# First maxima row on ScalarE's queue, half of the first q on GpSimd's, third head's q and two gate/up tiles further on

## The chip, the cores and the metric

The kernel runs on one core of one Trainium2 chip. The metric is the device time of one execution in microseconds (us). Three runs of the kernel before gave 1214.02, 1212.59 and 1212.71 us, a median of 1212.71. One further execution was profiled.

## The reference

What is computed, cut to what matters (2048 tokens, width 448, 16 heads of 28, hidden width 1792; all in float32):

```python
x = A_x                                             # (1, 2048, 448)
g = sigmoid((x * gate_w).sum(-1, keepdims=True))
q, k, v = split(x @ wqkv)                           # 16 heads of 28
a = softmax(q @ k.T * 28 ** -0.5) @ v @ wo          # per head, then joined
gate, up = x @ W_gate, x @ W_up                     # (2048, 1792)
b = (gate * (gate > 0) * up) @ W_down
return g * a + (1 - g) * b
```

## The kernel before

**Numbers.** Almost every matmul operand is split into a high part and the remainder (`act_high` and `low`: ScalarE casts, VectorE or GpSimd subtracts), and the products of the parts are accumulated, 11 matmuls (`NT`) for a full width of 448. A row block of 512 tokens is `tb` 0 to 3, and `X[tb]` holds its two parts, each a tile of 1 MB.

**Stages.** (1) Preparation: `qk` units project a block of q and k columns, and send both parts to the DRAM array `qk_d` (every second unit through the staging tile `K[2]`, the others through the tiles `rl` and `h`, all stores on GpSimd's queue). `load_k(h)` and `load_q(h)` bring one head back, q once for each of two halves of the rows and each of two parts, in four transfers of 224 KB. `vproj` units make V, and between their matmuls stand the matmuls of `smax`, which find the largest score of each query of heads 0 and 1, so that the later exponentials cannot overflow. `smax_end(h)` transposes these maxima, splits them into the two halves of the tile `mh`, and writes them as two rows into the head's q tile `Q[h]`: scores then come out with their maximum already subtracted. (2) Attention: 32 rounds, each an order string (`R0` to `R31`), in which each letter is one step: `s` a pair of score matmuls and ScalarE's copy or exponential of them, `m` an `smax`, `x` one matmul of a remaining qk unit or a gate/up unit, and so on. (3) The rest: `down` steps (12 matmuls each, one for each 128 hidden units and 512 tokens), the last `gate_up` tiles, the output projection `wout`, and the mix with the gate.

**What sets the order.** The schedule is by hand: every engine and every DMA queue runs its instructions in the order in which the code issues them, and a DMA on a queue waits for its data before those behind it can go. SP issues nearly all DMAs, POOL (GpSimd) the stores of the preparation and the spills.

**Preparation around the change.** The list `mixed` has 19 units: three `qk`, then 16 `vproj`, blocks 3 down to 0. At step `n` of it some side work is issued first: loads of heads 1 and 2, the splits of two pieces of the raw weights (`split_w(*w3)`, `split_w(*w2)`, four or two casts on ScalarE, the remainders on POOL), and `spill_x(tb, r)`, which stores one part of `X[tb]` to the DRAM array `x_d` by POOL's queue. The spills clear the way twice. The third q tile, `Q2`, lies where the second part of `X[3]` was, so the load of head 2's q waits for spill (3, 1). And the first score tiles `P` lie where the others were: slot 0 at (3, 0), slots 1 and 2 at (2, 0) and (2, 1), slots 3 and 4 at (1, 0) and (1, 1). `EARLY` places eight score pairs in the last five `vproj` units; the first four of these need no maxima, the fifth needs the row of head 0. `fetch_f` loads raw gate/up weights.

**End around the change.** Of the 56 gate/up tiles (14 for each block) the rounds do 52 (`done`), and the other four stand in the list `todo` of stage 3. Each reads weights (`wg`, two buffers of 896 KB) that were split once and are loaded again from DRAM (`ws_d`); `load_f(i + 2)` is issued when tile `i` is done. Its result goes to DRAM (`spill_h`), to be read by a `down` step of the fourth block. A `down` step reads the two parts of one hidden tile, `hh`, made by `split_d` from `hk` or `hr`.

Of the kernel before, what the change touches and what calls it, by code (L numbers as in the profile page):

```python
# [18 lines left out]
P = 128  # L19
# [3 lines left out]
DH = 28  # L23
G = 4
GD = G * DH
F = 1792
NF = F // P
NB = 4
# [83 lines left out]
def gated_mix_kernel(ctx, tc, x, wq, wo, wgu, wd, out):  # L112
    nc = tc.nc
# [7 lines left out]
    def f32(ap):  # L121
        return ap.bitcast(F32)
# [21 lines left out]
    def ps_x(name):  # L144
        return psum.tile([P, TB], F32, tag="x", bufs=2, name=name)
# [7 lines left out]
    def low(dst, src, high):  # L153
        nc.vector.tensor_tensor(dst, src, f32(high), op=OP.subtract)  # L154
# [5 lines left out]
    qk_d = dram.tile([2 * D, 2, S + P], F32, name="qk_d")[:, :, :S]  # L160
# [17 lines left out]
    def last_q(name, dt=F32R):  # L178
        return vp.tile([P, 4, TB], dt, name=name, tag="Q2", bufs=1)
# [9 lines left out]
    Q = {}  # L189

    def rows_kq(h):

        g, j = divmod(h, 4)
        k = 2 * GD * g + (DH * j if g else 2 * DH * j)
        return k, k + (GD if g else DH)

    def load_k(h):
        a = rows_kq(h)[0]
        k = qk_d[a:a + DH].rearrange("d r t -> (d r) t")
        for a in (0, 2 * DH):  # L200
            nc.sync.dma_start(f32(K[h % 3])[a:a + 2 * DH], k)

    def load_q(h):
        Q[h] = QS[h % 3].rearrange("p j t -> p (j t)")
        if h > 2:
            nc.sync.dma_start(f32(Q[h])[GD:GD + 2], f32(Q[h])[GD + 2:GD + 4])
        q = rows_kq(h)[1]
        for a in range(2):
            for r in range(2):
                nc.sync.dma_start(f32(Q[h])[2 * DH * a + r:2 * DH * (a + 1):2], qk_d[q:q + DH, a])  # L210

    MX, M = {}, {}
    def raw(v):
# [29 lines left out]
    def smax_end(h):  # L243

        pt = ps_x(f"mt_{h}")
        n = NU[h]
        nc.tensor.transpose(pt[:n, :P], M.pop(h), ident)
        mh = keep.tile([n, 2, P], F32R, name=f"mh_{h}", tag="mh", bufs=1)
        nc.scalar.activation(mh[:, 0], pt[:n, :P], AF.Copy)
        low(mh[:, 1], pt[:n, :P], mh[:, 0])  # L250
        for r in range(2):
            nc.sync.dma_start(f32(Q[h])[GD + r:GD + r + 1, :n * P], f32(mh)[:, r])

    AT, QUAD, slots = {}, {}, iter(range(10 ** 6))

# [104 lines left out]
    def fetch_f(i):  # L360

        if i >= NF:
            return
        WR[i] = fe.tile([P, 2, 4, P], F32, name=f"wgr_{i}", tag="wgr", bufs=2)
        nc.sync.dma_start(WR[i], wgu[i % NF])
# [10 lines left out]
    with tc.tile_pool(name="qkv", bufs=1) as pa:  # L376
        W = pa.tile([P, 7, VO + VC], F32R, name="W")

        def load_w(c):
            c0, c1 = c * 2 * GD, (c + 1) * 2 * GD if c < G + 1 else 2 * D + VC  # L380
            wr = pa.tile([P, 4, 2 * GD + 2], F32, name=f"wr_{c0}", tag="wr", bufs=2)[:, :, :c1 - c0]
            if c > 0:
                nc.sync.dma_start(wr, wq[:, :, c0:c1])
            return wr, c0, c1

        def split_w(wr, c0, c1, low=low):

            n, k = c1 - c0, VO - 2 * GD
            if c0 == 2 * GD:
                ways = [(W[:, :, c0:VO], wr[:, :, :k]), (WB[0][:, :, :n - k], wr[:, :, k:])]  # L390
            elif c0 == 4 * GD:
                k = 2 * P - (c0 - VO)
                ways = [(WB[0][:, :, 2 * P - k:], wr[:, :, :k]), (WB[1][:, :, :n - k], wr[:, :, k:])]
            elif c0 == 6 * GD:
                ways = [(WB[1][:, :, 2 * P - n:], wr)]
            else:
                ways = [(W[:, :, c0 - 2 * D + VO:c1 - 2 * D + VO], wr)]
            for w, r in ways:
                act_high(w[:, 0:3], r[:, 0:3])
                low(w[:, 3:6], r[:, 0:3], w[:, 0:3])  # L400
            for w, r in ways:
                act_high(w[:, 6], r[:, 3])
                low(w[64:, 6], r[64:, 3], w[64:, 6])
# [39 lines left out]
        def spill_x(tb, r):  # L443
            nc.gpsimd.dma_start(x_d[tb, r], f32(X[tb][r]))
# [95 lines left out]
        split_w(*w4)  # L540
        load_k(0)
        load_q(0)

        mixed = [(qk, 3, 1), (qk, 2, 2), (qk, 3, 2)]
        mixed += [(vproj, tb, t) for tb in range(NB - 1, -1, -1) for t in range(4)]
        spills = dict(zip((7, 8, 9, 10, 11, 12, 14, 16), ((3, 0), (2, 0), (2, 1), (1, 0), (3, 1), (1, 1), (0, 0), (0, 1))))
        m, first, ahead = 0, 6, MAXIMA
        for n, (f, *a) in enumerate(mixed):
            if n == 0:
                split_w(*w5)  # L550
            if n == 1:
                w3 = load_w(3)
            if n == 2:
                load_k(1)
                load_q(1)
            if n == 3:
                w2 = load_w(2)
            if n == 4:

                nc.gpsimd.memset(f32(K[2])[96:128], -1.0)  # L560
            if n == 7:
                load_k(2)
            if n == 8:
                split_w(*w3, pool_low)
            if n == 10:
                split_w(*w2, pool_low)
            if n == 13:
                QS.append(last_q("Q2"))
                for i, j in ((GD, 12), (GD + 12, 4)):
                    nc.sync.dma_start(f32(QS[2])[i:i + j].rearrange("p j t -> p (j t)"), Q[1][GD + 2:GD + 2 + j].bitcast(F32))  # L570
                load_q(2)
            if n == len(mixed) - 6:
                fetch_f(0)
                fetch_f(1)
            if n in spills:
                spill_x(*spills[n])

            among, was = [], m
            while n >= first and m < (n + 1 - first) * ahead / (len(mixed) - first):
                among.append((smax, m))  # L580
                m += 1
            news = [(score,) for back in EARLY if back == len(mixed) - n]
            for k, c in enumerate(news):
                among.insert(2 * k + 1, c)
            f(*a, among=among)

            if 0 in M and was > ends[0]:
                smax_end(0)
# [18 lines left out]
    done = (starts[-1] - QP) // (2 * NT)  # L607
# [178 lines left out]
    for v, order in enumerate(ROUNDS):  # L786
# [4 lines left out]
        for o in order:  # L791
# [12 lines left out]
            elif o == "x":  # L804
                i, half, n = passes.pop(0)
# [18 lines left out]
            elif o == "n":  # L824
                if v % 2 and v < 2 * H - 1:
                    smax_end(v // 2 + 1)
            elif o == "w":
                ready = -(-max(0, starts[v + 2] - QP) // NT)
                ready = min(ready + ready % 2, 2 * NF)
                while parts < ready and parts // 2 - 2 in finished:  # L830
                    split_f(parts // 2, act_high, pool_low, (parts % 2,))
                    parts += 1
                    if parts % 2 == 0:
                        fetch_f(parts // 2 + 1)
            elif o == "b":
                block_min()
            elif o == "A":
                all_max()
            elif o == "g":
                take_max()  # L840
            elif o == "N":
                if v > 1 and v % 2:
                    normalise(v // 2 - 1)
            elif o in "eE":
                take_exp(o == "E")
            elif o in "cf":
                rescale(v, "cf".index(o))
            elif o == "D":
                split_wd(len(early))
                early.append(o)  # L850
            elif o in "PQ":
                pv(v, "PQ".index(o))
# [10 lines left out]
    def load_wo():  # L863
        r = pf.tile([P, 4, TB], F32, name="wor", tag="on0", bufs=2)
        nc.sync.dma_start(r[:, 0:3, :D], wo_d[0:3 * P].rearrange("(c p) n -> p c n", p=P))  # L865
        for a in (0, 64):
            nc.sync.dma_start(r[a:a + 64, 3, :D], wo_d[3 * P:])  # L867
        return r[:, :, :D]
# [82 lines left out]
    def down(i):  # L951
# [6 lines left out]
        if f == NF - 1:  # L958
# [8 lines left out]
    todo = [(fetch_w, 4), (fetch_h, 4), (fetch_w, 5), (fetch_h, 5), (split_d, 0), (row_sums, H - 1), (split_d, 1),  # L967
            (fetch_w, 6), (fetch_w, 7), (lambda: wor.append(load_wo()),), (fetch_h, 6), (gate_up, done), (spread, H - 1),
            (split_wd, 4), (fetch_w, 8), (split_wd, 5), (fetch_w, 9), (fetch_h, 7), (gate_up, done + 1)]
    for i in range(NB * NF):  # L970
        if 5 < i + 3 < NF:
            todo += [(split_wd, i + 3), (fetch_w, i + 7)]
        if i + 2 < NB * NF:
            todo.append((split_d, i + 2))
        if i >= 2:
            todo.append((fetch_h, i + 6))
        todo.append((down, i))
        if done + 2 + i < NB * NF:
            todo.append((gate_up, done + 2 + i))

    def before(i, *new):
        n = todo.index((down, i))
# [51 lines left out]
```

## Time and profile before

| | |
|---|---|
| median of three runs | 1212.71 us |
| the profiled execution | 1216.88 us |
| its span, first to last instruction | 1215.0 us |
| mean granted TensorE clock | 0.990 |
| TensorE (PE) busy | 1188.5 us |
| VectorE (DVE) busy | 896.1 us |
| ScalarE (ACT) busy | 878.8 us |
| GpSimd (POOL) busy | 741.5 us |
| DMA | 188.86 MB, mean 155 GB/s |

The profile gives one execution. A timeline row has start, duration, engine, line, operation, output and input, count, and in brackets how long the engine was idle ahead of it and what ended that. SPq, ACTq and POOLq are DMA issues on those engines' queues. A line such as "PE s L341 <- DMA Q<-mh" says that TensorE's matmul of tile `s` in line 341 waited for the DMA that writes `Q` from `mh`. Names leave buffer numbers out. The clock column is the share of the full TensorE clock that was granted.

### The profile page before, as it was taken

To read this page: it belongs to the slowest core of one execution; us is meant where nothing else is said; L and a number is where in the kernel's file an instruction comes from. 1 tells how busy PE (TensorE), PEld (TensorE's weight loads), DVE (VectorE), ACT (ScalarE), POOL (GpSimd) and SP (SyncE) were. 2 spreads that over 40 slices of the span, in tenths; PEclk is the share of its full clock that TensorE was granted. 3 is DMA by queue.
4 is the path that set the end of the run, shared out by engine and by line. 5 is a ranking of instruction groups with operands and counts; after the bars stand their busy time and mean duration, and the time that the engine had idled before them with its cause. 6 is when DMAs were issued, how large, how long until landed. Compare 5 with 4: busy or idle time off the path is not lost. (4 is left out here: it accounts for less than half of the span.)

```text
span 1215.0 us, 16951 instructions
## 1 busy us (share of the span) xinstructions
PE 1188.5 (98%) x6183; PEld 824.6 (68%) x6183; DVE 896.1 (74%) x1173; ACT 878.8 (72%) x1018; POOL 741.5 (61%) x323
## 2 busy tenths in 40 slices
PE   9996999999999999999999999999999998999998
PEld 6784666666666666666666566666666665899987
DVE  5484888888888888989888898989888551443342
ACT  5234788999999888888888888888888983422121
POOL 5320767789888777767776766667687773321020
PEclk9997999999999999999999999999999998999999
DMA  8983555754454645343446435153544337543342
GB/s 307 271 329 115 183 178 178 233 166 156 148 149 156 191 139 149 109 134 109 126 119 215 124 115 156 40 156 98 161 128 156 125 119 240 155 147 111 121 126 77
DMA packets 70655, 188.86 MB, mean 155 GB/s; under 512 B 13946, under 2 KB 20546, under 8 KB 65666
## 3 DMA queue, kind: packets, MB, share of 16 engines
q1 hardware_dynamic: 65756, 167.78, 44.9%
q0 software_dynamic: 4384, 19.53, 4.3%
q8 instruction: 49, 0.80, 0.3%
q10 hardware_dynamic: 432, 0.46, 0.1%
q14 instruction: 34, 0.28, 0.1%
HBM read 126.96 MB, written 60.96 MB: 155 GB/s over the span
## 5 line engine op out<-in xcount | busy, mean ns | idle before, releaser
L320 POOL TENSOR_TENSOR P<-P,rm 128x2048 f32<-128x2048 f32 x102 | 470.6, 4633 | 117.9 <-DVE rm L314 85.1
L644 PE MATMUL gu<-X,wg 128*128 128x512 f32 x1232 | 366.2, 399 | 5.8 <-DMA wg<-ws_d 5.8
L239 DVE TENSOR_REDUCE mx<-sm 128x1 f32<-128x1024 f32 x256 | 304.5, 1217 | 71.2 <-PE sm L235 69.2
L341 PE MATMUL s<-Q,K 128*128 128x512 f32 x1024 | 320.7, 403 | 12.6 <-DMA Q<-mh 10.9
L644 PEld LDWEIGHTS gu<-X,wg 128*128 128x128 f32 x1232 | 232.1, 189 | 77.2 <-issue 19.6
L341 PEld LDWEIGHTS s<-Q,K 128*128 128x128 f32 x1024 | 182.7, 188 | 92.1 <-issue 17.1
L347 ACT ACTIVATE P<-s 128x1024 f32<-128x1024 f32 x204 | 202.0, 1028 | 39.6 <-PE s L341 37.1
L703 PE MATMUL po<-P,V 128*32 128x512 f32 x1640 | 229.9, 595 | 0.0
L345 ACT ACTIVATE P<-s 128x1024 f32<-128x1024 f32 x206 | 201.8, 1032 | 28.6 <-PE s L341 26.7
L331 ACT ACTIVATE P<-P 128x1024 f32<-128x1024 f32 (+1 forms) x154 | 202.1, 1344 | 1.4 <-POOL P L320 1.1
L291 DVE SCALAR_TENSOR_TENSOR r<-s,r 128x1024 f32<-128x1024 f32 x124 | 151.8, 1224 | 20.8 <-ACT P L347 10.2
L235 PE MATMUL sm<-K,Q 128*128 128x512 f32 x520 | 161.4, 399 | 2.2 <-DMA Q<-qk_d 2.1
L703 PE MATMUL po<-V 128*32 128x512 f32 x408 | 136.8, 594 | 0.0
L703 PEld LDWEIGHTS po<-P,V 128*32 128x32 f32 x1640 | 60.8, 109 | 110.6 <-issue 107.4
L320 POOL TENSOR_TENSOR V<-V,rm 128x2048 f32<-128x2048 f32 x24 | 111.2, 4634 | 23.1 <-DVE rm L314 12.2
L235 PEld LDWEIGHTS sm<-K,Q 128*128 128x128 f32 x520 | 94.2, 189 | 34.5 <-issue 5.0
L148 ACT ACTIVATE hh<-hr 128x512 fp32r<-128x512 f32 x52 | 32.7, 631 | 113.2 <-PE acc L938 111.0
L154 DVE TENSOR_TENSOR hh<-hr,hh 128x512 fp32r<-128x512 f32 x52 | 45.2, 875 | 78.2 <-ACT hh L148 78.2
L938 PE MATMUL acc<-WD,hh 128*128 128x448 f32 x480 | 100.1, 366 | 0.4 <-DVE hh L154 0.3
L938 PEld LDWEIGHTS acc<-WD,hh 128*128 128x128 f32 x480 | 90.0, 188 | 8.7 <-DVE hh L154 1.2
L306 DVE TRANSPOSE_TENSOR_REDUCE mn<-r 128x32 f32<-128x1024 f32 x63 | 77.9, 1237 | 1.2
L291 DVE SCALAR_TENSOR_TENSOR r<-s,P 128x1024 f32<-128x1024 f32 x50 | 61.2, 1223 | 23.6 <-ACT P L347 23.1
(92 smaller groups left out, 1136.4 us busy)
## 6 DMA issues: line engine op xcount, KB each, us to landing
wg<-ws_d SPq DMA_DIRECT2D x42, 896.0 KB
K<-qk_d SPq DMA_DIRECT2D x32, 448.0 KB
Q<-qk_d SPq DMA_DIRECT2D x64, 224.0 KB
X<-x_d SPq DMA_DIRECT2D x56, 256.0 KB
h_d<-h SPq DMA_DIRECT2D x56, 256.0 KB
hr<-h_d SPq DMA_DIRECT2D x52, 256.0 KB
ws_d<-wg SPq DMA_DIRECT2D x14, 896.0 KB
x_d<-X POOLq DMA_DIRECT2D x8, 1024.0 KB, 10.5
```

The source lines that it names most:

```text
L235: nc.tensor.matmul(ps[:, c, :], Q[h][:, u * P:(u + 1) * P], K[h % 3][:, k0:k0 + TB], start=True, stop=True)
L239: nc.vector.tensor_reduce(to, ps, axis=AX.XY, op=OP.max)
L291: nc.vector.scalar_tensor_tensor(r, ps, -1.0, before, op0=OP.mult, op1=OP.min)
L306: nc.vector.tensor_reduce(MN[:, 1:3], R2.pop((v, j)).rearrange("p a (b r) -> p a b r", r=32), axis=AX.X, op=OP.min, apply_transpose=True)
L320: nc.gpsimd.tensor_tensor(QUAD[q], QUAD[q], m, op=OP.subtract)
L331: nc.scalar.activation(q, q, AF.Exp, scale=-SCALE)
L341: nc.tensor.matmul(ps[:, c], K[h % 3][:, k * P:(k + 1) * P], Q[h][:, j * TB:(j + 1) * TB], start=True, stop=True)
L345: nc.scalar.activation(dst, ps, AF.Exp, scale=SCALE)
L347: nc.scalar.activation(dst, ps, AF.Copy, scale=-1.0)
L644: nc.tensor.matmul(ps, WS[i][:, s, a], xf(i // NF, b), start=(n == 0), stop=(n == NT - 1))
L703: nc.tensor.matmul(po[32 * j:32 * j + 32], V[:, h // 4 % 2, k, h % 4], AT.pop((v, k, j)), start=(k == k0), stop=(k == k0 + NK // 2 - 1))
L938: nc.tensor.matmul(ACC[i // NF][t][:, :D], HH[i][:, a, t * P:(t + 1) * P], wd_high_low(f, b), start=(f == 0 and n == 0), stop=(f == NF - 1 ...
```

## The change

Five edits. The first head's q is loaded by two queues: its first half (`a` = 0, two of four transfers) by GpSimd, the second by SP. The two row transfers of `smax_end(0)` are issued by ScalarE's queue; those of later heads stay on SP. Spill (3, 1) becomes the second of the eight, and the last two come at steps 16 and 17 in place of 14 and 16. The side work moves on: the two weight splits from steps 8 and 10 to 12 and 14, the load of head 2's q from 13 to 17, `fetch_f` from 13 to 18. In stage 3 the last two gate/up tiles stand behind down steps 2 and 4 instead of 0 and 1.

```diff
@@ load_q
-                nc.sync.dma_start(f32(Q[h])[2 * DH * a + r:2 * DH * (a + 1):2], qk_d[q:q + DH, a])
+                queue = nc.sync if h or a else nc.gpsimd
+                queue.dma_start(f32(Q[h])[2 * DH * a + r:2 * DH * (a + 1):2], qk_d[q:q + DH, a])
@@ smax_end
-            nc.sync.dma_start(f32(Q[h])[GD + r:GD + r + 1, :n * P], f32(mh)[:, r])
+            (nc.sync if h else nc.scalar).dma_start(f32(Q[h])[GD + r:GD + r + 1, :n * P], f32(mh)[:, r])
@@ preparation
-        spills = dict(zip((7, 8, 9, 10, 11, 12, 14, 16), ((3, 0), (2, 0), (2, 1), (1, 0), (3, 1), (1, 1), (0, 0), (0, 1))))
+        spills = dict(zip((7, 8, 9, 10, 11, 12, 16, 17), ((3, 0), (3, 1), (2, 0), (2, 1), (1, 0), (1, 1), (0, 0), (0, 1))))
...
-            if n == 8:
+            if n == 12:
                 split_w(*w3, pool_low)
-            if n == 10:
+            if n == 14:
                 split_w(*w2, pool_low)
-            if n == 13:
+            if n == 17:
                 QS.append(last_q("Q2"))
...
-            if n == len(mixed) - 6:
+            if n == len(mixed) - 1:
                 fetch_f(0)
                 fetch_f(1)
@@ todo
-        if done + 2 + i < NB * NF:
-            todo.append((gate_up, done + 2 + i))
+        if i % 2 == 0 and 0 < i and done + 1 + i // 2 < NB * NF:
+            todo.append((gate_up, done + 1 + i // 2))
```

SP's queue in the preparation, from the load of head 0's q on (`Q_107`, `Q_108` and `Q_684` are the q tiles of heads 0, 1 and 2, `wr` raw weights of qk, `wgr` raw gate/up weights, `mh` the maxima), before:

```order
L210 DMA Q_107<-qk_d 28x2048 x4
L383 DMA wr_401<-wq 128x4x224
L201 DMA K_105<-qk_d 56x2048 x2
L210 DMA Q_108<-qk_d 28x2048 x4
L383 DMA wr_442<-wq 128x4x224
L201 DMA K_106<-qk_d 56x2048 x2
L570 DMA Q_684<-Q_108 12x2048
L570 DMA Q_684<-Q_108 4x2048
L210 DMA Q_684<-qk_d 28x2048 x4
L365 DMA wgr_691<-wgu 128x1024
L365 DMA wgr_693<-wgu 128x1024
L252 DMA Q_107<-mh_755 1x12x128 x2
```

The same place of the change (head 2's q is now `Q_810`, and line numbers behind 209 are one higher):

```order
L211 DMA Q_107<-qk_d 28x2048 x2
L384 DMA wr_401<-wq 128x4x224
L201 DMA K_105<-qk_d 56x2048 x2
L211 DMA Q_108<-qk_d 28x2048 x4
L384 DMA wr_442<-wq 128x4x224
L201 DMA K_106<-qk_d 56x2048 x2
L571 DMA Q_810<-Q_108 12x2048
L571 DMA Q_810<-Q_108 4x2048
L211 DMA Q_810<-qk_d 28x2048 x4
L366 DMA wgr_849<-wgu 128x1024
L366 DMA wgr_851<-wgu 128x1024
L375 DMA qk_d<-rl_qk_0_933 128x512
```

Two of head 0's q loads have gone to POOL's queue (there behind the last store that they read, ahead of the stores of the three mixed `qk` units), and the two rows of maxima to ScalarE's, behind its cast of `mh`; the rest keeps its order on SP.

POOL in the preparation, from the first spill on (`x_d_0_78<-X_3` is spill (3, 0), `x_d_1_79<-X_3` is (3, 1), and so on; `wb` are the weight splits, `v_d` the stores of V), before:

```order
L444 DMA x_d_0_78<-X_3_121 128x2048
L157 TENSOR_TENSOR wb_114<-wr_401,wb_114 128x3x224
L157 TENSOR_TENSOR wb_114<-wr_401,wb_114 64x224
L444 DMA x_d_0_76<-X_2_123 128x2048
L444 DMA x_d_1_77<-X_2_124 128x2048
L157 TENSOR_TENSOR wb_113<-wr_442,wb_113 128x3x192
L157 TENSOR_TENSOR wb_114<-wr_442,wb_114 128x3x32
L157 TENSOR_TENSOR wb_113<-wr_442,wb_113 64x192
L157 TENSOR_TENSOR wb_114<-wr_442,wb_114 64x32
L444 DMA x_d_0_74<-X_1_125 128x2048
L488 DMA v_d_80<-V 128x512
L488 DMA v_d_81<-V 128x512
```

And of the change:

```order
L445 DMA x_d_0_78<-X_3_121 128x2048
L445 DMA x_d_1_79<-X_3_122 128x2048
L445 DMA x_d_0_76<-X_2_123 128x2048
L445 DMA x_d_1_77<-X_2_124 128x2048
L489 DMA v_d_80<-V 128x512
L489 DMA v_d_81<-V 128x512
L445 DMA x_d_0_74<-X_1_125 128x2048
L157 TENSOR_TENSOR wb_114<-wr_401,wb_114 128x3x224
L157 TENSOR_TENSOR wb_114<-wr_401,wb_114 64x224
L445 DMA x_d_1_75<-X_1_126 128x2048
L157 TENSOR_TENSOR wb_113<-wr_442,wb_113 128x3x192
L157 TENSOR_TENSOR wb_114<-wr_442,wb_114 128x3x32
```

Four spills now stand in a row, and five stand ahead of the first split; the second split follows the sixth.

ScalarE at the beginning of stage 3 (`rl` is the relu of a gate/up tile, `hh` the cast for a down step, `WD` and `WO` casts of weights), from the relu of the second of the four tiles on, before:

```order
L660 ACTIVATE rl_9014<-gu_8989 128x512
L148 ACTIVATE hh_9020<-hk_8229 128x512
L660 ACTIVATE rl_9062<-gu_9039 128x512
L148 ACTIVATE hh_9068<-hk_8229 128x512
L148 ACTIVATE WO<-wor 128x1344
L148 ACTIVATE WO<-wor 128x448
L660 ACTIVATE rl_9115<-gu_9092 128x512
L148 ACTIVATE hh_9121<-hr_8918 128x512
L148 ACTIVATE WD<-wdr_8933 128x448
L148 ACTIVATE hh_9142<-hr_8922 128x512
```

And of the change:

```order
L661 ACTIVATE rl_9014<-gu_8989 128x512
L148 ACTIVATE hh_9020<-hk_8229 128x512
L148 ACTIVATE hh_9039<-hk_8229 128x512
L148 ACTIVATE WO<-wor 128x1344
L148 ACTIVATE WO<-wor 128x448
L148 ACTIVATE hh_9063<-hr_8918 128x512
L661 ACTIVATE rl_9103<-gu_9080 128x512
L148 ACTIVATE WD<-wdr_8933 128x448
L148 ACTIVATE hh_9113<-hr_8922 128x512
L594 ACTIVATE e<-zt 128x16
L148 ACTIVATE WD<-wdr_8935 128x448
L148 ACTIVATE hh_9139<-hr_8941 128x512
```

The third tile's relu now follows the casts of down steps 2, 3 and 4 in place of step 2's alone, and the fourth tile's stands behind these rows.

## The prediction

> **What bounds the kernel now.** I read the page first, then the waits of TensorE, then windows around each of its stops, then each queue's timeline there.
>
> ```profile
> span 1215.0 us, 16951 instructions
> ...
> PE 1188.5 (98%) x6183; PEld 824.6 (68%) x6183; DVE 896.1 (74%) x1173; ACT 878.8 (72%) x1018; POOL 741.5 (61%) x323
> ```
>
> TensorE is busy for 98% of the span, so an edit can pay only where TensorE stands still or is slowed. Its waits over the whole span name these places (engine, line, what it waited for: us in total, times, longest):
>
> ```profile
> PE s L341 <- DMA Q<-mh: 10.9, 1, 10.9
> PE gu L644 <- DMA wg<-ws_d: 5.8, 1, 5.8
> PE sm L235 <- DMA Q<-qk_d: 2.1, 1, 2.1
> PE warm_ps L507 <- DVE warm L504: 1.2, 1, 1.2
> ```
>
> Three waits hold 18.9 us; nothing else is above 1.2 us. Each of the three is touched by one part of the change. The windows show each wait, the matmuls behind it, and the same set of matmuls elsewhere (window, length, busy time and count of PE, PEld, DVE, ACT, POOL; then the granted clock, DMA share, GB/s):
>
> ```profile
> 46.16:48.30 2.14, 0.00 (x1) 0.03 (x1) 0.00 (x0) 0.00 (x0) 0.42 (x1) 1.00 0.87 323
> 48.30:52.29 3.99, 3.98 (x11) 3.43 (x12) 2.08 (x2) 0.00 (x0) 1.38 (x1) 0.57 1.05 272
> 57.20:59.56 2.36, 2.36 (x12) 2.07 (x11) 2.25 (x3) 0.26 (x1) 2.28 (x3) 1.00 0.99 206
> 91.22:102.15 10.93, 0.01 (x1) 0.03 (x1) 0.87 (x1) 0.00 (x0) 0.00 (x0) 0.59 0.74 220
> 102.15:107.41 5.26, 5.26 (x15) 4.41 (x15) 1.23 (x1) 1.47 (x2) 0.00 (x0) 0.55 0.00 0
> 107.41:110.44 3.03, 3.03 (x16) 2.63 (x15) 1.44 (x2) 2.10 (x4) 0.00 (x0) 1.00 0.00 0
> 1021.66:1027.49 5.83, 0.00 (x0) 0.03 (x1) 0.00 (x0) 0.00 (x0) 0.00 (x0) 0.79 1.04 348
> 1027.49:1034.69 7.20, 7.20 (x23) 5.71 (x23) 0.00 (x0) 0.00 (x0) 1.28 (x1) 0.70 0.78 255
> 1037.12:1042.28 5.16, 5.16 (x24) 4.14 (x23) 2.18 (x2) 0.57 (x2) 0.00 (x0) 1.00 0.32 91
> 300.00:900.00 600.00, 599.49 (x3255) 378.03 (x3257) 527.17 (x691) 526.97 (x566) 446.36 (x154) 1.00 0.45 137
> ```
>
> A wait costs twice. Behind each the clock is about 0.6, and the matmuls take longer than the like stretch at full clock: 3.99 - 2.36 = 1.63 us, 5.26 - 3.03 = 2.23 us, 7.20 - 5.16 = 2.04 us. So the first wait is worth 2.14 + 1.63 = 3.8 us, the second 10.93 + 2.23 = 13.2, the third 5.83 + 2.04 = 7.9. From 300 to 900 us TensorE is full at clock 1.00: what is gained in the preparation stays gained.
>
> **The row of maxima (second wait).** Head 0's first scores need the row `mh`. Its halves exist early and leave late (start, us, engine, line):
>
> ```profile
> 80.88 0.27 ACT L249 ACTIVATE mh<-mt 12x128 fp32r<-12x128 f32 x1
> ...
> 82.17 0.27 DVE L154 TENSOR_TENSOR mh<-mt,mh 12x128 fp32r<-12x128 f32 x1
> ...
> 81.99 2.21 SPq L570 DMA_DIRECT2D Q<-Q  x2
> 84.25 7.93 SPq L210 DMA_DIRECT2D Q<-qk_d  x4
> 92.23 1.47 SPq L365 DMA_DIRECT2D wgr<-wgu  x2
> 93.81 1.63 SPq L252 DMA_DIRECT2D Q<-mh  x2
> ...
> SPq L570 <- DMA x_d<-X: 28.1, 1, 28.1
> ```
>
> Done at 82.44, issued from 93.81 to 95.44: SP sat 28.1 us at the third head's buffer, which waited for a spill of X, then issued six DMAs for that buffer and two weight loads ahead of the row. On ScalarE's queue the row passes all eight. Two issues at SP's 0.8 us each end by 83.3; TensorE wants the row at 91.22, 7.9 us later. A row's landing on ScalarE's queue is not in this trace. On SP it took 102.15 - 95.44 = 6.7 us with two weight loads just ahead of it, which would do; the longest of the spills to DRAM is the bound above:
>
> ```profile
> DMA to landing us min/median/max: 4.3/10.5/14.7
> ```
>
> At 14.7 us TensorE would still wait 14.7 - 7.9 = 6.8 us and lose the slow stretch: 9 of the 13.2 us stay lost. Six KB sit nearest to the 6.7 us row, so I take no wait: **-13.2**. Cover: 7.9 us. What the issues hold up on ScalarE:
>
> ```profile
> 83.07 1.02 ACT L347 ACTIVATE P<-s 128x1024 f32<-128x1024 f32 x1 [1.92 <-PE s L341]
> ```
>
> It had waited 1.92 us for TensorE before 83.07; the second issue, held until 82.44, may delay this copy by 0.2 us, which that idle time absorbs for the next. It stands in the allowance below.
>
> **Head 0's q (first wait).** SP loads it behind K, in four issues; POOL issues the stores these loads wait for:
>
> ```profile
> 32.59 0.68 POOL L475 DMA_DIRECT2D qk_d<-K  x1 [1.99 <-DVE K L154]
> 34.41 0.56 POOL L374 DMA_DIRECT2D qk_d<-rl_qk  x1 [1.14 <-ACT rl_qk L148]
> ...
> 47.88 1.80 POOL L560 MEMSET K<- 32x2048 f32 x1 [7.12 <-DMA qk_d<-K]
> 53.33 1.07 POOL L488 DMA_DIRECT2D v_d<-V  x2 [3.65 <-ACT zt L485]
> ...
> 35.83 0.79 SPq L201 DMA_DIRECT2D K<-qk_d  x2
> 36.66 3.32 SPq L210 DMA_DIRECT2D Q<-qk_d  x4
> ```
>
> Two K loads of 448 KB and four of q at 224 KB, 1792 KB, are issued from 36 us and let TensorE go at 48.30: 12.3 us. With two q loads taken out, SP's share is 1344 KB: 9.2 us at that pace, 45.2, before TensorE's 46.16. POOL's pair must wait for the store issued at 32.59, so until about 35.8; with issues like its other 0.6 us ones it is out by 37.1. At the spills' median of 10.5 us it lands at 47.6, at their shortest of 4.3 at 41.4. Both directions are open: at 14.7 us (51.8) TensorE waits 3.5 us longer than now, at 9 us or less it waits for nothing. The pair is smaller than a spill and nothing is queued ahead of it on POOL's queue, so I take it as gone but for 0.3 us: **-3.5**. POOL's wait puts the store of 34.41 and those behind it back by up to 2.8 us; they feed the memset at 47.88, and the v_d store behind it has 3.65 us idle ahead of it, which covers that.
>
> The Trainium skill speaks against this part: DMA: Bandwidth & Descriptors, "Issuing engines are not separate DMA queues", says that transfers of all issuers share the same 16 engines and interleave, so a second issuer only saves issue time. The trace has DMA busy at 0.87 in the wait, which fits. By that rule the 3.8 us stay and the sum falls to 19.6 us; it is a rival below.
>
> **Third head's q, spills, splits.** Four issues of q, two copies and two weight loads now stand behind later code on SP, but their blocker, X's spill (3,1), moves from fifth to second on POOL and is no longer held behind the weight splits. Nothing needs that q before the second round string, nor the weight loads before the fourth; the last two spills, up to two steps later, free X for reloads that the first round issues only after its first four units. If that cover went, TensorE would wait for the rest of a transfer there. The two splits move four steps on; their first reader, at L652, comes at 110.90, some 30 us after. The risk is the second split's raw load:
>
> ```profile
> 69.97 1.23 ACT L148 ACTIVATE wb<-wr 128x576 fp32r<-128x576 f32 x4 [6.88 <-DMA wr<-wq]
> ...
> 76.16 0.55 ACT L484 ACTIVATE V<-v 128x448 f32<-128x448 f32 x1 [2.58 <-PE v L480]
> ...
> 78.79 1.03 ACT L347 ACTIVATE P<-s 128x1024 f32<-128x1024 f32 x1 [2.02 <-PE s L341]
> ...
> 64.00:68.00 4.00, 4.00 (x20) 3.52 (x19) 3.76 (x4) 0.00 (x0) 0.00 (x0) 1.00 0.94 393
> ```
>
> Now it lands at 69.97 amid three spills of 1 MB; then up to two more are ahead, each 1 MB / 393 GB/s = 2.7 us: 70 to 75.4. After the 3.5 us gained above, ScalarE must start the first score copy at 75.3, so the four casts (1.23 us) must start by 74.1. The cost lies between nothing and 75.4 - 74.1 = 1.3 us, more if the spills' overlap is worse; I take **+0.5** for this and the delayed copies. Behind the casts on ScalarE queue the copies that free PSUM, and for those TensorE waits.
>
> **Two gate and up tiles (third wait).**
>
> ```profile
> 1019.06 2.60 PE L938 MATMUL acc<-K,hh 128*128 128x448 f32 x12
> 1027.49 7.36 PE L644 MATMUL gu<-X,wg 128*128 128x512 f32 x22 [5.83 <-DMA wg<-ws_d]
> ...
> 1047.14 14.75 PE L938 MATMUL acc<-WD,hh 128*128 128x448 f32 x72
> ...
> 1019.50 0.38 SPq L629 DMA_DIRECT2D wg<-ws_d  x1
> ...
> 1020.50 0.68 DVE L154 TENSOR_TENSOR hh<-hk,hh 128x512 fp32r<-128x512 f32 x1
> ```
>
> One down step of 12 matmuls is 14.59 / 6 = 2.43 us (start 1047.14 to the next group at 1061.73). The tile whose weights land at 1027.49 now follows three steps, not one: 2 x 2.43 = 4.86 us of the 5.83 are filled. The third step reads the `hh` done at 1021.2, so it is ready. 0.97 us of wait stays, since the weights are still issued at 1019.50 behind the same DMAs. If the clock holds through that, the part is worth 7.87 - 0.97 = **-6.9**. The second moved tile's load and the stores moved behind it have two steps more, which hide them.
>
> **The sum**: 3.5 + 13.2 + 6.9 - 0.5 = 23.1 us. The profiled execution took 1216.88 us around a span of 1215.0, so it would take 1193.8. Its time is 4.2 us above the runs' median of 1212.71; I put the same gain on the median: **1189.6 us**.
>
> **The rivals.**
> (a) Head 0's q is bound by the DMA engines, and the first wait stays: 1189.6 + 3.5 = 1193.1. For it: share 0.87 and 323 GB/s in the wait. Against: POOL's pair now stands ahead of stores that competed with it.
> (b) The raw load of the second split is late: with all five spills ahead, twice 2.7 us more, 1.3 + 5.4 = 6.7 us at most, so 1190.4 to 1195.8. For: the 6.88 us wait it already causes.
> (c) The 0.97 us left at the third wait still drops the clock: +2.0, 1191.6. For: a wait of only 2.14 us did so. The Trainium skill, TensorE: Matmul & The Clock Gate, Part 1, gives an idle window of about 3.4 us before half rate; by that 0.97 us is free, yet 2.14 us should have been free too, and the trace shows 0.57.
> (d) The row lands in 14.7 us: +9.0, 1198.6.
> (e) Slower: the wait for the row turns into one for the score slots. The scores write where X stood, and the two spills that now follow the splits or the v_d stores free the last of them. TensorE would reach that slot near 95 us, so they pay back all 23.1 us from a landing of about 118 us on, and every us beyond is lost: at 120.5, 1215.1. Before, the last spill of all left POOL at 82.21,
>
> ```profile
> 82.21 0.54 POOL L444 DMA_DIRECT2D x_d<-X  x1
> ```
>
> and at 14.7 us it landed by 97: over 20 us short of that point.
> (f) It does nothing: the row's issue on ScalarE waits for something not seen here, and the other two gains go to (a) and to the next late load: 1212.7.
>
> **How the numbers follow.** Forecast 0.58, (a) 0.13, (b) 0.12, (c) 0.09, (d) 0.04, (e) 0.02, (f) 0.02. The range takes the forecast with all three waits wholly gone (3.8 + 13.2 + 7.9 = 24.9: 1187.8, and 1 us for what the unprofiled runs differ), and above it (a), (b), (c) and most of (a) with (b): 1186.8 to 1197.5. About 0.2%, 2.4 us, is what a measurement of this kernel can tell from no change: faster 0.96 (all but e and f), same 0.02, slower 0.02.
>
> **What would show it.** TensorE's list of waits should lose `Q<-mh` and `Q<-qk_d` and keep about 1 us of `wg<-ws_d`; the granted clock should have no dip near 90 us or after the tile at the end; the row's issue on ScalarE's queue should stand within 2 us of the VectorE half. (b) would show as ScalarE waiting for `wr<-wq` over 1 us with TensorE behind it, (e) as score copies waiting for `x_d<-X`. I am wrong if a new TensorE wait of over 3 us stands anywhere before 130 us.

## The result and the profile after

The changed kernel took 1195.72 us in the median of four runs (1194.10 to 1197.05), the kernel before 1213.37 us (four runs, 1212.59 to 1215.43; three of them are those given ahead of the change). The ratio is 0.9851, with a 95% interval of 0.9833 to 0.9870: faster by 17.7 us. The forecast of 1189.6 us was 6.1 us too low; the time lies inside the range of 1186.8 to 1197.5.

The profiled execution of the changed kernel took 1196.28 us. Its page, the span and the engines' busy time:

```profile
span 1194.5 us, 16947 instructions
...
PE 1183.0 (99%) x6183; PEld 821.9 (69%) x6183; DVE 896.9 (75%) x1173; ACT 879.0 (74%) x1018; POOL 743.3 (62%) x325
```

The span is 20.5 us shorter, and TensorE's busy time fell by 5.5 us for the same 6183 matmuls, most of it time at a low clock (5.9 us behind the three waits before, 1.65 us behind one now). TensorE's waits over the whole span (engine, line, what it waited for: us in total, times, longest):

```profile
PE gu L645 <- DMA wg<-ws_d: 2.1, 1, 2.1
PE sm L236 <- DMA Q<-qk_d: 1.4, 1, 1.4
PE warm_ps L508 <- DVE warm L505: 1.2, 1, 1.2
PE s L342 <- DVE mx L240: 0.9, 1, 0.9
```

The row of maxima, 10.9 us before, is gone from the list. The other two large waits are smaller but not gone, and a new one of 0.9 us stands at line 342. Windows around the two waits that are left (first to last number: window, length, busy time and count of PE, PEld, DVE, ACT, POOL, granted clock, DMA share, GB/s):

```profile
45.75:47.14 1.39, 0.00 (x2) 0.03 (x1) 0.00 (x0) 0.00 (x0) 0.00 (x0) 1.00 0.90 357
47.14:50.05 2.91, 2.91 (x14) 2.52 (x15) 2.12 (x2) 0.27 (x1) 0.86 (x1) 1.00 0.96 366
1011.79:1013.94 2.15, 0.00 (x1) 0.01 (x1) 1.93 (x3) 0.02 (x1) 0.00 (x0) 1.00 1.02 290
1013.94:1020.74 6.80, 6.80 (x23) 5.39 (x24) 0.00 (x0) 0.00 (x0) 1.27 (x1) 0.75 0.88 290
1025.60:1030.75 5.15, 5.15 (x23) 4.14 (x22) 0.33 (x1) 0.00 (x0) 0.00 (x0) 1.00 0.83 252
```

Behind the wait for q the clock now holds at 1.00. Behind the wait for the gate and up weights it falls to 0.75, and the tile takes 6.80 us where the like tile takes 5.15: 1.65 us more.

Where the gain arose can be read from when the same matmuls start in both traces. The first `qk` matmul of line 652 (653 after) starts at 110.90 before and 96.16 after: 14.74 us gained in the preparation. The first gate and up tiles of the last stage start at 1008.65 and 993.92: 14.73, so the 900 us between gave and took nothing. The first `wo` matmul starts at 1061.73 and 1042.91: 18.82, so the two moved tiles gave 4.1 us. The last 1.7 us of the 20.5 come behind that place, where the change moved nothing; they are taken up at the end.

### The profile page after: what moved, and what is told of

Its sections match the earlier page's. It is cut to its first block, busy times and chain, and to the rows that moved or that the text cites. A ratio compares the mean times of both kernels' runs of the same rounds, so it can differ in the third digit from the quotient of the medians.

```text
span 1194.5 us, 16947 instructions
## 1 busy us (share of the span) xinstructions
PE 1183.0 (99%) x6183; PEld 821.9 (69%) x6183; DVE 896.9 (75%) x1173; ACT 879.0 (74%) x1018; POOL 743.3 (62%) x325
## 5 line engine op out<-in xcount | busy, mean ns | idle before, releaser
L332 ACT ACTIVATE P<-P 128x1024 f32<-128x1024 f32 (+1 forms) x154 | 202.1, 1344 | 1.4 <-POOL P L321 1.1
L154 DVE TENSOR_TENSOR hh<-hr,hh 128x512 fp32r<-128x512 f32 x52 | 46.6, 900 | 74.1 <-ACT hh L148 73.8
```

The source lines that it names most:

```text
L332: nc.scalar.activation(q, q, AF.Exp, scale=-SCALE)
```

## The experiments

Twelve kernels ran: nine new ones, and the kernel before, the changed kernel and the fastest version once more. They ran four at a time, those of one group on the same chip with the kernel before beside them. The kernel before had medians of 1215.93, 1217.00 and 1215.98 us in the three groups (single runs 1212.69 to 1218.72), so kernels of different groups are compared by their ratio to it.

### Which of two edits brought the row forward

The change takes the row off SyncE's queue, and it also moves the third head's q, which had blocked that queue. Two kernels do one of the two. First, the kernel before with the row alone moved:

```diff
-            nc.sync.dma_start(f32(Q[h])[GD + r:GD + r + 1, :n * P], f32(mh)[:, r])
+            (nc.sync if h else nc.scalar).dma_start(f32(Q[h])[GD + r:GD + r + 1, :n * P], f32(mh)[:, r])
```

> The kernel before with one edit: the first row of maxima goes by ScalarE's queue. Theory (a late issue on SP was the whole of the second wait): TensorE's 10.9 us wait for the row is gone although the third head's q, the spills and the splits stand as before; a wait of about 0.9 us appears at the score matmul two pairs earlier, as in the changed kernel; the first and third waits stay at about 2.1 and 5.8 us. Time: before less 12.3, about 1201 us (1199.5 to 1203). Rival (the moved spills and the moved q were needed, since the score slots or the third head's q come late otherwise): a wait of 3 us or more for a spill or for the row stays near 90 us, time above 1204.

It took 1204.59 us, 0.9902 of the kernel before (0.9885 to 0.9919). Its waits of TensorE:

```profile
PE gu L644 <- DMA wg<-ws_d: 6.8, 1, 6.8
PE sm L235 <- DMA Q<-qk_d: 1.6, 1, 1.6
...
PE s L341 <- DVE mx L239: 0.9, 1, 0.9
```

Second, the changed kernel without its other three parts: the row and all of the first q on SyncE, the two tiles where they were, and only the third head's q, the spills, the splits and the fetches moved:

```diff
-                queue = nc.sync if h or a else nc.gpsimd
+                queue = nc.sync
...
-            (nc.sync if h else nc.scalar).dma_start(f32(Q[h])[GD + r:GD + r + 1, :n * P], f32(mh)[:, r])
+            nc.sync.dma_start(f32(Q[h])[GD + r:GD + r + 1, :n * P], f32(mh)[:, r])
...
-        if i % 2 == 0 and 0 < i and done + 1 + i // 2 < NB * NF:
-            todo.append((gate_up, done + 1 + i // 2))
+        if done + 2 + i < NB * NF:
+            todo.append((gate_up, done + 2 + i))
```

> The changed kernel with the row of maxima back on SP's queue, the first q all on SP, and the two gate and up tiles where they were: only the third head's q, the spills, the splits and the weight loads are moved. SP now has the row ahead of the third head's q. Theory (a late issue was the whole of the second wait): the row is issued within 1 us of its VectorE half, the 10.9 us wait is gone, and so is the 0.9 us wait, as ScalarE issues nothing: before less 13.2, about 1200 us (1198.5 to 1202). Rival (the row needs a queue of its own, as transfers of SP delay it): a wait of 2 us or more for the row stays, time above 1203.

It took 1203.80 us, ratio 0.9893 (0.9878 to 0.9909). Its timeline at the row, and its waits:

```profile
79.18 0.27 ACT L250 ACTIVATE mh<-mt 12x128 fp32r<-12x128 f32 x1
79.47 2.04 SPq L253 DMA_DIRECT2D Q<-mh  x2
80.46 0.27 DVE L154 TENSOR_TENSOR mh<-mt,mh 12x128 fp32r<-12x128 f32 x1
```

```profile
PE gu L645 <- DMA wg<-ws_d: 7.1, 1, 7.1
PE sm L236 <- DMA Q<-qk_d: 2.1, 1, 2.1
```

Either edit alone takes the wait for the row away. In the first kernel SyncE still sits 27.4 us at the third head's buffer, but the row is not behind it. In the second the row leaves SyncE as soon as its first half is there, since the third head's loads now stand behind it. Both rivals fall by the lists of waits, that the row needs its own queue and that it needs the moves as well. (The second kernel makes its moves together; which of them would do alone was not tried.) In the changed kernel the two edits do the same work twice.

The times themselves missed: 1199.5 to 1203 and 1198.5 to 1202 us were expected, and the rivals had theirs above 1204 and 1203. The expectations start from the kernel before at 1213.37 us, which took 1215.93 in this group; the gains are 11.3 and 12.1 us where 12.3 and 13.2 were expected.

The list of the first kernel has the 0.9 us wait at line 341 and that of the second has not. So the changed kernel was run again with the row back on SyncE, beside the changed kernel itself:

> The changed kernel itself, as the mark for the other runs of this row on the same chip. Earlier its ratio to the kernel before was 0.985. Theory: the third wait is not 1 us, as the prediction had it, but 2.1 us, and loses some 1.7 us more by a lower clock, because the tile's weights land 9 us after their issue; so its profile has again a wait for wg of 1.8 to 2.4 us with the tile behind it at 6.8 to 7.2 us. Rival: the 2.1 us of the first profile were one execution's accident; then the wait is near 1 us and the tile takes 5.3 us.

> The changed kernel with the row of maxima issued by SyncE again. Theory: the move of the third head's q and spills alone has emptied SyncE's queue ahead of the row, so the row wait stays gone and the 0.9 us wait for the VectorE maximum at s_4_3 goes too: changed minus 0.9 us, 0.1% (0.3 to 1.3 us less). Rival: the row needs ScalarE's queue, and a row wait of 2 us or more returns: changed plus 2 to 13 us.

The changed kernel took 1194.88 us (1193.39 to 1196.44; ratio 0.9825, 0.9807 to 0.9843), with the row on SyncE 1192.70 us (1191.97 to 1193.67; ratio 0.9807, 0.9790 to 0.9824). The difference is 2.2 us where 0.9 was expected. The profiles place 0.95 us of it. From the end of the wait for q to the start of the last stage, the four profiles with the row on ScalarE and a full clock there take 946.67 to 946.95 us, the six with the row on SyncE, the third head's q moved and a full clock 945.75 to 945.95. The other 1.2 us of the medians can't be placed by one profile each. The rival, that a wait for the row returns, falls: with the row on SyncE, TensorE's list has neither that wait nor the 0.9 us one, and its largest for scores is

```profile
PE s L342 <- DVE r L292: 0.6, 2, 0.3
```

The 0.9 us wait stood in all five profiles with the row on ScalarE and in none of the seven with the row on SyncE and the third head's q moved. The timeline of the changed kernel around it shows what the issues hold up (first the scores and their copy on ScalarE, then the late scores on TensorE):

```profile
78.50 2.17 ACTq L253 DMA_DIRECT2D Q<-mh  x2
...
79.66 0.65 PE L342 MATMUL s<-Q,K 128*128 128x512 f32 x2
...
80.72 1.02 ACT L348 ACTIVATE P<-s 128x1024 f32<-128x1024 f32 x1 [2.29 <-PE s L342]
```

```profile
82.95 0.73 PE L342 MATMUL s<-Q,K 128*128 128x512 f32 x2 [0.91 <-DVE mx L240]
```

With the row in its queue, ScalarE sits at the second issue until the VectorE half is done and the issue is out at 80.67, and the copy behind it starts only then, 0.4 us after its scores are done at 80.31; with the row on SyncE it starts 0.04 us after them. The built programs differ in one more thing, the PSUM buffer that the next scores get (TensorE's instructions in program order, `-` with the row on SyncE, `+` the changed kernel):

```
-L342 MATMUL s_4_3_773<-Q_107,K_104 128x512 [waits Activation_49]
+L342 MATMUL s_4_3_773<-Q_107,K_104 128x512 [waits DVE_49]
```

So the scores that had waited for a ScalarE copy now take a buffer that VectorE's maximum frees, and VectorE frees it 0.9 us late. That the row's place is the cause is shown; that it acts through the choice of buffer is read from the program and was not tried by itself.

### What is left of the wait for the weights

The second run of the changed kernel, already given, had its tile behind a wait of 1.55 us, and no loss of clock (start, us, engine, line):

```profile
1012.96 5.41 PE L645 MATMUL gu<-X,wg 128*128 128x512 f32 x22 [1.55 <-DMA wg<-ws_d]
1018.21 2.63 PE L939 MATMUL acc<-K,hh 128*128 128x448 f32 x12
```

The theory's 1.8 to 2.4 us with the clock down again was wrong, and so was the rival's 1 us. The weights landed 8.8 us after their issue at 1004.17, and in the first profile 9.0 us after theirs at 1004.90. Two kernels move the tiles further on, behind down steps 4 and 6, counted from 0 like the 2 and 4 of the change (the expectations say fourth and sixth); the second also has the row on SyncE:

```diff
-        if i % 2 == 0 and 0 < i and done + 1 + i // 2 < NB * NF:
-            todo.append((gate_up, done + 1 + i // 2))
+        if i in (4, 6):
+            todo.append((gate_up, done + i // 2))
```

> The changed kernel with the last two gate and up tiles behind down steps 4 and 6 instead of 2 and 4. Theory (what is left of the third wait is only the landing of the weights, and the clock fell behind it): no wait for the weights, clock 1.00 from 1000 to 1040 us, 2.1 + 1.8 = 3.9 us less than the changed kernel, about 1191.8. Rival (the down steps then run into hidden tiles or weights of their own that are late): a wait for hh or a weight split of 2 us or more takes its place, 1194 to 1196.

> The changed kernel with the row on SyncE and the two gate and up tiles behind the fourth and sixth down step. Theory: both gains add, 0.9 us and 3.9 us (2.1 us of wait and 1.8 us of clock), less the 0.8 us that TensorE waited for hh in the run with these tiles: changed minus 4.0 us (3 to 5), 0.978 of the kernel before. Rival: the two are not independent, because the stages between absorb what the first gains; then it is changed minus 3 us or less.

The first took 1193.43 us, ratio 0.9814 (0.9800 to 0.9829). Its waits:

```profile
PE s L342 <- DVE mx L240: 0.9, 1, 0.9
PE acc L939 <- DVE hh L154: 0.8, 1, 0.8
...
PE sm L236 <- DMA Q<-qk_d: 0.5, 1, 0.5
```

```profile
1139.32 5.08 PE L939 MATMUL acc<-WD,hh 128*128 128x448 f32 x22 [0.75 <-DVE hh L154]
```

The wait for the weights is gone, but about 1191.8 us had been expected. A wait for `hh` has come, 0.8 us, in the last block but one, some 120 us behind the moved tiles. The 120 matmuls of which these are the last 22 take 25.7 us there, 24.3 in the changed kernel's first profile and 24.7 to 25.4 in the twelve others, so the place of the tiles alone does not make it. The second took 1192.26 us (1191.77 to 1193.62; ratio 0.9805, 0.9788 to 0.9822): 2.6 us below the changed kernel of its group where 4.0 (3 to 5) were expected, in number what the rival had said. The expectation took 1.8 us of lost clock for granted, which the changed kernel's profile in that group did not have. In this group the tiles gave 0.4 us of median over the kernel with the row alone on SyncE, and 1.9 us of profiled span (1191.9 to 1190.0), but the profiled executions were the slowest of four and the fastest of four.

One step less, behind steps 3 and 5 (third and fifth in the expectations), the row on SyncE as well:

```diff
-        if i % 2 == 0 and 0 < i and done + 1 + i // 2 < NB * NF:
-            todo.append((gate_up, done + 1 + i // 2))
+        if i in (3, 5):
+            todo.append((gate_up, done + (i + 1) // 2))
```

> As the last one, but the tiles behind the third and fifth down step, one step of 2.43 us later than in the changed kernel. Theory: the weights land 9.0 to 9.4 us after their issue, and one step fills 2.43 of the 2.1 us: no wait over 0.3 us, no clock drop, and the 0.8 us wait for hh of the run with steps 4 and 6 is gone or smaller: changed minus 4.0 to 5.0 us. Rival: the landing varies by more than that step leaves, and the wait and the clock drop return in some executions: changed minus 0.9 to 2 us, with a wg wait of over 0.5 us in the profile.

It took 1191.53 us, ratio 0.9797 (0.9781 to 0.9814): 3.35 us below the changed kernel of its group, a little under the expected 4.0 to 5.0. Its five runs lie between 1191.32 and 1191.86. TensorE runs from the steps into the tile without a stop:

```profile
1002.93 9.89 PE L939 MATMUL acc<-K,hh 128*128 128x448 f32 x48
1012.66 5.30 PE L645 MATMUL gu<-X,wg 128*128 128x512 f32 x22
1017.80 5.03 PE L939 MATMUL acc<-WD,hh 128*128 128x448 f32 x24
```

This is the fastest version that ran. A second time, in another group, it took 1192.90 us, ratio 0.9813 (0.9800 to 0.9827), again with no wait for the weights:

> The kernel with the row on SyncE and the tiles behind the third and fifth step once more, as the mark for the next two. Theory: 0.979 to 0.981 of the kernel before, its runs within 1.5 us of each other, since no wait long enough for the clock is left; no wg wait over 0.3 us. Rival: the wg wait comes back in this execution.

### GpSimd's half of the first q

The changed kernel with all four loads of head 0's q on SyncE:

```diff
-                queue = nc.sync if h or a else nc.gpsimd
+                queue = nc.sync
```

> The changed kernel with the first q all on SP again. Theory (the second issuer brings the q about 0.8 us forward, and the clock's fall hangs on whether the wait passes some length between 1.4 and 2.1 us): the first wait is back at about 2.1 us, the clock falls behind it, and the time is 2.3 us above the changed kernel's, about 1198. Rival (the transfers share the same engines, so the issuer changes nothing, and the 1.4 us against 2.1 us was a difference between two executions): wait 1.4 us or less, no fall of the clock, 1195.7 us.

It took 1197.67 us, ratio 0.9847 (0.9830 to 0.9863), which can't be told from the 0.9851 and 0.9825 of the changed kernel: the times are inconclusive, since one comparison scatters by more than this part is worth. Its profile has the wait of 1.95 us and the half clock behind it that were expected. The same edit was made on the fastest version, with that version beside it (1192.90, 1191.78 to 1192.95), and another with all four loads on GpSimd (`nc.sync if h else nc.gpsimd`):

> The last kernel with all of the first q on SyncE. Theory: GpSimd's half shortens the wait for q from 1.6 to 2.2 us to 0.5 to 1.4 us, and keeps it out of the range in which the clock falls: here the mark plus 1.0 to 1.3 us where the clock holds and plus 2.5 to 3 us where it falls, so a median 1 to 3 us above the mark and a wider spread. Rival: all six loads share the DMA engines, the wait stays, and the time is within 0.5 us of the mark.

> The same kernel with all four loads of the first q by GpSimd. Theory: in the profiles the last of the q loads to land is SyncE's pair, issued behind K; on GpSimd all four are issued by about 37.6 us and land by 45.5 to 46.5 us: the wait goes to 0 to 0.5 us, the mark minus 0.5 us. Rival: the bytes set the landing, not the issuer: the wait stays 0.5 to 1.4 us and the time is that of the mark within 0.3 us.

All on SyncE: 1194.63 us (1194.38 to 1194.98). All on GpSimd: 1192.55 us (1191.92 to 1193.36). So GpSimd's half is worth 1.7 us of median here, and its other half nothing that can be told. The timelines with POOL's stores of `rl_qk` and `h_qk` (256 KB each), all on SyncE:

```profile
34.20 0.56 POOL L375 DMA_DIRECT2D qk_d<-rl_qk  x1 [1.14 <-ACT rl_qk L148]
...
35.66 0.54 POOL L375 DMA_DIRECT2D qk_d<-h_qk  x1 [0.91 <-DVE h_qk L154]
...
36.45 3.32 SPq L211 DMA_DIRECT2D Q<-qk_d  x4
...
48.45 0.70 PE L236 MATMUL sm<-K,Q 128*128 128x512 f32 x2 [2.50 <-DMA Q<-qk_d]
48.98 1.32 PE L481 MATMUL v<-W,X 128*128 128x450 f32 x4
```

Half and half (the fastest version, second run):

```profile
35.46 1.03 POOL L211 DMA_DIRECT2D Q<-qk_d  x2 [2.71 <-DMA qk_d<-K]
...
36.14 1.70 SPq L211 DMA_DIRECT2D Q<-qk_d  x2
...
36.47 0.57 POOL L375 DMA_DIRECT2D qk_d<-rl_qk  x1
...
37.03 0.55 POOL L375 DMA_DIRECT2D qk_d<-h_qk  x1
...
46.75 0.70 PE L236 MATMUL sm<-K,Q 128*128 128x512 f32 x2 [1.09 <-DMA Q<-qk_d]
47.29 0.98 PE L481 MATMUL v<-W,X 128*128 128x450 f32 x4
```

All on GpSimd:

```profile
35.93 2.01 POOL L211 DMA_DIRECT2D Q<-qk_d  x4 [2.70 <-DMA qk_d<-K]
...
47.34 0.70 PE L236 MATMUL sm<-K,Q 128*128 128x512 f32 x2 [1.21 <-DMA qk_d<-h_qk]
```

In the third the profile, which infers what ended a wait, names a store of GpSimd's queue; the matmul reads only K and Q.

In the first two profiles the last stage starts at 995.89 and 992.59 us, 3.30 us apart: the wait is 1.41 us longer, and the half clock behind it costs 1.58 us (from the first of these pairs of `sm` matmuls to the sixth 8.46 us, against 6.88). The half-and-half profile then lost 1.5 us of that again near its end, at a wait for `hh` and in slower matmuls (the last section), so the difference in median says less than the part is worth.

The end of the last q issue is 39.77, 37.84 and 37.94 us, and TensorE goes on 8.7, 8.9 and 9.4 us after it. Over all fourteen profiles this gap is 7.8 to 9.4 us. The split took 1.9 us off the end of the issuing; moving the other half as well shortens it no further, and the expected 0 to 0.5 us of wait did not come. The 1.21 us of wait and 0.35 us of time are near what the rival had said, that the bytes set the landing. The expected wider spread with all q on SyncE did not come either (0.60 us; the version beside it had 1.17).

One rival was not separated. GpSimd's pair waits 2.71 us in its queue for the K store, and the two stores behind it, which with all q on SyncE are issued ahead of q's loads, now come behind GpSimd's pair and the start of SyncE's. Those 512 KB take 1.3 us at the 393 GB/s of the prediction's window (an estimate), about as much as the wait fell in the mean (1.2 us). That the two loads on GpSimd brought the landing forward is shown; whether by earlier issuing or by holding back the stores is open.

### The kernel before, profiled again

> The kernel before, profiled a second time. Theory: its first profile caught the shortest landing of the late gate and up weights (8.0 us) of all runs, and a slow last block; a second profile has a wg wait of 6.5 to 7.5 us in place of 5.8, the waits for q and for the row as they were (1.6 to 2.2 us, 9.5 to 10.5 us with the clock down behind each), and the 168 matmuls of the last block near 34.1 us. Rival: the 5.8 us are this kernel's own, and 8.0 us is its landing again.

It took 1216.19 us beside 1215.98 us of the same kernel (ratio 1.0005, 0.9996 to 1.0015). Its waits:

```profile
PE s L341 <- DMA Q<-mh: 9.5, 1, 9.5
PE gu L644 <- DMA wg<-ws_d: 6.2, 1, 6.2
PE sm L235 <- DMA Q<-qk_d: 2.3, 1, 2.3
```

The wait for the weights is 6.2 us, between the 5.8 of the first profile and the 6.5 to 7.5 expected, with 9.1 us from issue (1016.75) to landing (1025.84) where the first had 8.0. The landing took 1.1 us longer and the wait grew by only 0.3, since the issue came 10.1 us behind the start of the stage and not 10.9. So the rival falls, that 8.0 us is this kernel's own landing. The last 168 matmuls took 34.2 us (1176.05 to 1210.25) where the first profile has 34.9: as expected.

## Why the prediction was right, and where it was off

**First wait, forecast -3.5, in the profile -2.4.** It was worth 3.8 us; 1.39 us of wait is left and no lost clock. In the second profile of the changed kernel 0.70 us is left, so -3.1. The step that failed is the pace: "SP's share is 1344 KB: 9.2 us at that pace, 45.2". The landing did not shrink with SyncE's bytes: TensorE went on between 46.45 and 47.14 us in the seven profiles with the split, 7.8 to 9.4 us after the last issue in all fourteen. The six profiles with all q on SyncE waited 1.64 to 2.50 us (mean 2.10), the seven with the split 0.51 to 1.39 (mean 0.91).
Rival (a), that the wait stays, falls. The Trainium skill, DMA: Bandwidth & Descriptors, "Issuing engines are not separate DMA queues", says that a second issuer saves only the time of issuing, usually a small part of the transfer. The trace does not contradict it; what the prediction got wrong was to read that as nothing saved. In the mean of these profiles the last issue ended 1.7 us sooner (38.1 against 39.8), and the wait was 1.2 us shorter (0.91 against 2.10); the clock fell in four of the six and in none of the seven. Whether the earlier issuing did this, or the stores that were held back, is open.

**Second wait, forecast -13.2, in the profile -12.3.** The row left at once and landed in time: with it on ScalarE the first scores of head 0 start at 89.43 without a wait, so rivals (d) and (f) fall. The 0.9 us missing are the new wait at line 342, whose price the allowance had at 0.2 us of hidden delay: the copy was held 0.4 us, and TensorE lost 0.9. The forecast put the gain down to ScalarE's queue alone. The two runs of one edit each show that the moves around the third head's q do it as well, and without the 0.9 us.

**The allowance, +0.5 us for the second split's raw load, was not needed.** ScalarE cast it at 73.94 without a wait in the profile, just inside the prediction's 74.1, and rival (b) did not come. Nor did rival (e): TensorE has no wait over 1.4 us before the last stage. SyncE still waits for a spill, 13.0 us where it was 28.1, but nothing that is needed soon stands behind it.

**Third wait, forecast -6.9, in the profile -4.1.** This is the term that was most off. The order of the work was right, three steps of 2.43 us ahead of the tile, but the landing was read from one execution. From issue to landing the tile's weights took 8.0 us there, and 9.1, 9.3, 9.4, 9.0, 9.2, 8.8 and 8.6 in the seven other profiles in which TensorE waited for them. At the median of the eight, 9.07, the wait left is 0.97 + 1.08 = 2.05 us and not 0.97; 2.15 were measured. That put it where rival (c) applies, and the clock fell (1.65 us). In the second profile the wait was 1.55 us, the clock held, and the part gave 7.9 - 1.55 = 6.3 us. Why the first profile's landing was the shortest is open.

**The sum.** 2.4 + 12.3 + 4.1 = 18.8 us in the profile, against 23.1: 2.8 us from the third wait, 1.1 from the first, 0.9 from the second, less the 0.5 us allowed.

**From the profile to the median.** The forecast put the profile's gain on the median. The profiled execution of before was 3.5 us above the 1213.37 us of its four runs, that of the changed kernel 0.6 us above its 1195.72. The 1.7 us of span that came behind the first `wo` fit this: the 120 matmuls around a wait of 0.31 us for `hh`, which stood in before's profile and not in after's, took 25.3 us against 24.3, and before's last steps ran 2% slower than after's (timeline of TensorE, before and then after):

```profile
1176.39 10.08 PE L938 MATMUL acc<-K,hh 128*128 128x448 f32 x48
1186.31 24.96 PE L938 MATMUL acc<-WD,hh 128*128 128x448 f32 x120
```

```profile
1156.43 9.89 PE L939 MATMUL acc<-K,hh 128*128 128x448 f32 x48
1166.15 24.48 PE L939 MATMUL acc<-WD,hh 128*128 128x448 f32 x120
```

The change does not touch these steps. Across groups the gain of the same change in medians was 17.7 us (1213.37 to 1195.72) and 22.1 us (1217.00 to 1194.88). Both lie below the 23.1, but how much of the 6.1 us by which the forecast missed is the three terms (4.3 us net in the profile) and how much the scatter of executions, one comparison of four runs each does not tell.

## What to carry to other kernels

Where a DMA is late because its queue is blocked, ask first what blocks the queue: moving the blocker freed it here as fully as another queue did, and the two issues, 2.2 us on the other queue, held up the copy behind them and cost TensorE 0.9 us. A landing time from one execution is a sample: a wait that is to be filled wants a spare step, and the step costs nothing where other work stands ready, while the wait that is left may cost almost as much again in clock (2.15 us of wait cost 1.65 more here). A second issuer can pay although the bytes stay the same: here two of four loads on GpSimd's queue shortened the wait by 1.2 us and kept the clock up, and that queue's own stores had to give way for it.

## What the runs showed of the hardware

The clock's fall after a wait of about 2 us is not decided by its length alone. In fourteen profiles the waits for q and for the weights between 1.87 and 2.50 us were seven: 1.87, 1.95, 2.14, 2.15, 2.32 and 2.50 were followed by matmuls at half clock, 2.06 was not. Eleven waits of 0.51 to 1.79 us were followed by none. The half clock lasted for some 3.3 us, here behind the weights in the changed kernel (window, length, PE busy and count, granted clock, DMA share, GB/s):

```profile
1012.00:1014.00 2.00, 0.06 (x1) 1.00 0.97 274
1014.00:1015.00 1.00, 1.00 (x3) 0.51 0.39 71
1015.00:1017.00 2.00, 2.00 (x6) 0.50 0.96 266
1017.00:1019.00 2.00, 2.00 (x9) 0.89 0.93 358
```

The Trainium skill, TensorE: Matmul & The Clock Gate, Part 1, gives free-running windows of about 3.4 us, and half rate after an idle one. The length of the slow stretch agrees. A fall after 1.87 us of wait does not fit a window that must be idle throughout; one that is idle for more than about half, 1.7 us, would fit all eighteen waits if those of 1.79 and 2.06 us lay across the border of two windows. This is argued from them and was not tested; the profiles do not show where the windows lie.

A second thing was not expected: stretches in which matmuls ran 2% slower at a granted clock of 1.00, 2.48 us for a step of 2.43. In the kernel before they held to the end from 1162 us on in one profile, and from about 1040 to 1167 us in the other, where the steps from 1040.15 on take 2.48 us (timeline of TensorE, the second profile):

```profile
1141.83 25.46 PE L938 MATMUL acc<-WD,hh 128*128 128x448 f32 x120
...
1185.77 24.48 PE L938 MATMUL acc<-WD,hh 128*128 128x448 f32 x120
```

The fastest version had such a stretch at its end in its second profile and none in its first, so they are not the kernel's. In three profiles the stretch that held to the end began behind a wait of 0.31 to 0.39 us for `hh` at the same matmul; in the second of the kernel before a stretch began without one. What brings them is open.
